# Block transposes on VectorE and moves by DMA for the gated tiles of a fused GateLoop and ELU kernel, with packed features and range tests on ScalarE

## The chip, the cores and the metric

The kernel runs on one core of a Trainium2 chip. A core has five engines with queues of their own: TensorE (PE, with its weight loads shown apart as PEld), VectorE (DVE), ScalarE (ACT), GpSimd (POOL) and SyncE (SP, which here only issues DMAs). They share an on-chip memory of 128 partitions (SBUF); matmul results land in PSUM. Each engine works through its queue in order and waits on semaphores. The metric is the device time of one execution in microseconds (us).

## The reference

A linear recurrence with complex, data-dependent decay, and a two-layer network with ELU behind it:

```python
# q, k, v, a_re, a_im: (batch 4, heads 8, seq 768, head_dim 48), float32
mag = np.sqrt(a_re * a_re + a_im * a_im)
scale = np.minimum(mag, 0.999) / (mag + 1e-06)
a_re_n, a_im_n = (a_re * scale, a_im * scale)
for t in range(S):
    new_re = ar * S_re - ai * S_im
    new_im = ar * S_im + ai * S_re
    S_re, S_im = (new_re + k_t v_t^T, new_im)
    y[:, :, t] = q_t . S_re
x = y as (3072 tokens, 8 * 48)
h = x @ w_in                       # 384 -> 2048
g = np.where(h > 0.0, h, np.exp(np.minimum(h, 0.0)) - 1.0)
out = g @ w_out                    # 2048 -> 384
```

The weights come as float64 words; all else is float32.

## The kernel before, in words

The work is cut into `NU` = 12 units, u = 0 to 11, each of two batch entries (`NB` = 2) and 128 time steps, with 8 heads. The recurrence is done in chunks of 64 steps: the running product of decays is turned into a length (E for q, F = 1/E for k) and an angle, whose cosine and sine stand side by side, so that each head has 48 cosine and 48 sine features. `scaled` multiplies q by E and k by F, and `gated` (L1014) multiplies both by cosine and sine. The result lies in two buffers that all units share, `kg` and `qg`, with time steps on the partitions. Each head takes 2 x 64 columns there, of which 2 x 48 are used and the rest is zero.

For the scores and for the product with the carried state the features must lie on the partitions. `transposed(u, key, n)` (L1034, L1035) does that for one of q or k and one batch entry: eight TensorE transposes of 128x128 into two PSUM tiles, and two ScalarE copies to SBUF. `small` (L1190) multiplies the turned k and q of all heads, in `state_products` (L1075) k and v, `masked` (L1198) applies the causal mask, and `valued_pe` and `carried_pe` (L1111, L1120) give y. ScalarE copies y out, small DMAs bring the heads into place (`seam`, L1241), and the network follows.

From the fourth unit on the network is computed with sums that save products. In `layer_of`, `mult` (L1507) makes twenty groups of matmuls with `w_in`, between which ScalarE (`kept` L1520, `low` L1528 and L1529) and VectorE (`joint` L1523, `whole_of` L1532) add parts together and apply the ELU; `folded` (L1348) prepares sums for `product` (L1370), fourteen groups of matmuls with `w_out`. The results leave by SP (L1398).

Two things are watched on the way. `noted` takes for each unit the smallest real part and the largest imaginary part of the decays (ScalarE with an accumulating output for the first three units, two VectorE reductions, L807 and L810, for the others). `test_fetch` and `test` (L677, L680, L691) read the float64 weights again in 48 pieces and take the smallest high word. `verdict` puts them together and decides whether a general version must run behind.

The order is written by hand: for the first units as a list, then as a plan in which every step has a time in slots, 16 slots to a unit (`put(at, step, ...)`), with a table `SHIFT` of small offsets. The steps are sorted by that time and recorded, and each engine's queue has its instructions in that order. In slots, unit u starts at r = 16 (u - 2). Its gates stand near r + 18 to r + 20, its turned tiles before r + 28.2, where `small` comes. The twenty groups of `mult` of the unit ahead take r + 20 to r + 28, so before the change the transposes of unit u stand among the `mult` groups of unit u - 1. SP issues the loads (`load_a`, `load_qk`, `load_v`), the tests' fetches and the stores in the order of the plan.

Of the kernel before, what the change touches and what calls it, by code (L numbers as in the profile page):

```python
# [505 lines left out]
def kernel(  # L506
# [53 lines left out]
    gates = {key: cst.tile([C, NB, H, 2, HP], FP32, name=key + "g") for key in ("k", "q")}  # L560
# [4 lines left out]
    seen = cst.tile([C, 2 * NU + NR], FP32, name="seen")  # L565
    least, smallest, most = seen[:, 0:NU], seen[:, NU : NU + NR], seen[:, NU + NR :]
    OFF = 3
    off = cst.tile([C, OFF, 2], FP32, name="off")
# [226 lines left out]
    def noted(u):  # L795


        ar, ai = nat[u]["ar"], nat[u]["ai"]
        if u < OFF:
            sq = nat[u]["sq"]  # L800
            for n, (x, scale, bias) in enumerate(((sq, 1.0, most_sq), (ar, -1.0, least_re))):
                nc.scalar.activation(
                    out=sq, in_=x, func=AF.Relu, scale=scale, bias=bias,
                    accum_out=off[:, u, n : n + 1],
                )
            return
        nc.vector.tensor_reduce(  # L807
            out=least[:, u : u + 1], in_=flat(ar), axis=mybir.AxisListType.X, op=ALU.min
        )
        nc.vector.tensor_reduce(  # L810
            out=most[:, u : u + 1], in_=flat(ai), axis=mybir.AxisListType.X, op=ALU.max,
            apply_absolute_value=True,
        )
# [135 lines left out]
    def ends(u):  # L949
# [17 lines left out]
        for i in range(2):  # L967
            nc.gpsimd.dma_start(
                out=x["T"][ds(i * HP, D)].rearrange("p n c h -> p (n c h)"),
                in_=x["ends"].rearrange("n c h d -> d (n c h)"),  # L970
            )
# [33 lines left out]
    def gated(u, part=None, keys=("k", "q")):  # L1005
# [4 lines left out]
        for key in keys if part is None else ("q", "k"):  # L1010
            eng = products(u) if key == "k" else nc.vector
            each = x[key][:, n : n + step].rearrange("p n h d -> p (n h) d")
            to = gates[key][:, n : n + step].rearrange("p n h i d -> p (n h) i d")
            eng.tensor_tensor(  # L1014
                out=to[:, :, :, 0:D], in0=each.unsqueeze(2).to_broadcast([C, step * H, 2, D]),
                in1=x["cs"][:, n * H : (n + step) * H], op=ALU.mult,
            )
# [5 lines left out]
    def transposed(u, key, n):  # L1023
        x = nat[u]
        if u >= PAIRED and key == "k" and n:
            o = new("cs", 1, [C, H, C])
        else:
            o = new(key + "t", 1 + (key == "q"), [C, H, C])
        x[key + "t", n] = o
        for h0 in range(0, H, 4):  # L1030
            t = work([C, 4, C])
            for h in range(4):
                of = gates[key][:, n, h0 + h].rearrange("p i d -> p (i d)")
                nc.tensor.transpose(t[:, h], of, ident)  # L1034
            nc.scalar.copy(out=o[:, h0 : h0 + 4], in_=t)  # L1035
# [19 lines left out]
    def state_products(u, n):  # L1055
# [12 lines left out]
        for h in range(H):  # L1068
            for c, g in enumerate(gs):
                k = gates["k"][ts(c, L), n, h]  # L1070
                parts = [(g[ts(i, HP), h], k[:, i]) for i in range(2)]
                if u == 0:
                    parts = [(g[:, h], k.rearrange("p i d -> p (i d)"))]
# [463 lines left out]
    def verdict():  # L1537

        ones, fit = value(1.0, "ones"), seen[:, 0 : NU + NR]
# [4 lines left out]
            out=least, in0=least, scalar1=LEAST_RE, scalar2=None, op0=ALU.is_ge  # L1544
        )
        nc.vector.scalar_tensor_tensor(
            out=least, in0=most, scalar=LEAST_RE, in1=least, op0=ALU.is_le, op1=ALU.mult
        )
        nc.vector.tensor_scalar(
            out=least[:, 0:OFF], in0=off[:, :, 0], scalar1=0.0, scalar2=None, op0=ALU.is_le  # L1550
# [34 lines left out]
    for n in range(2):  # L1585
        nc.gpsimd.tensor_copy(out=twice[:, ds(n * HP, D)], in_=ident[0:D, 0:D])
    for t in vn:
        nc.gpsimd.memset(t[:, :, HD:], 0.0)
    for t in gates.values():
        nc.gpsimd.memset(t[:, :, :, :, D:], 0.0)  # L1590
# [14 lines left out]
    def warm(n):  # L1605
# [13 lines left out]
        "gated()": 0.05, "gated(None, ('k',))": 0.5, "gated(None, ('k',))@5": -0.2,  # L1619
        "gated(None, ('q',))": 0.45, "gated(None, ('q',))@11": -0.2, "hidden(0,)": 0.05,  # L1620
# [164 lines left out]
    for u in range(2, NU):  # L1785
        r = (u - 2) * SLOTS
        put(r + (8 if u == PAIRED else 4.5 if u == PAIRED + 3 else 1.5), load_a, u)
        put(r + 8, load_v, u)
        put(r + 8, load_qk, u)
# [3 lines left out]
        else:  # L1793
            sq = (r + 7.2, r + 9.6) if u < PAIRED + 4 else (r + 5.08, r + 6)
            noting = r + (15.7 if u != PAIRED + 2 else 17.6)
# [87 lines left out]
```

## Time and profile before

| | |
|---|---|
| median of 3 runs | 645.02 us (643.92 to 645.48) |
| the profiled execution | 644.48 us, its span 642.8 us |
| clock granted to TensorE over that span | 0.996 |
| TensorE busy | 628.7 us |
| VectorE busy | 489.3 us |
| ScalarE busy | 428.5 us |
| GpSimd busy | 159.0 us |
| one unit, from one group of `mult` to the next unit's | 49.1 us |

The span is what the profiler saw between the first and the last instruction; the profiled execution's own time has some 1.7 us more around it. TensorE's row counts a matmul from its start to a modelled end, so a busy TensorE need not be at its peak. A row of a group gives the line, the engine, the operation, the tiles (output, then inputs) and their shapes, the count, and behind the bar the busy time in us and the mean ns of one.

### The profile page before, as it was taken

The numbers are of one execution on the slowest core, as the hardware profiler recorded it, in microseconds if no ns is written. First come the engines' busy times: TensorE is split into PE (matmuls) and PEld (weight loads), VectorE is DVE, ScalarE is ACT, GpSimd is POOL, SyncE is SP. The second block draws the span as 40 slices with busy tenths as digits, with TensorE's granted clock in tenths as the row PEclk, the third lists the DMA queues.
The fourth block names the chain that finished last, engine by engine and source line by source line (L and its number), as shares of the span: only waits on it lengthen the run. The fifth ranks groups of instructions, "written<-read, shape, count | busy, mean of one in ns | idle before, by whom it ended". The sixth has DMA issues, their size and how long they took to land.

```text
span 642.8 us, 17116 instructions
## 1 busy us (share of the span) xinstructions
PE 628.7 (98%) x7236; PEld 576.0 (90%) x7236; DVE 489.3 (76%) x777; ACT 428.5 (67%) x707; POOL 159.0 (25%) x201
## 2 busy tenths in 40 slices
PE   8899999999999999999999999999999999999996
PEld 5788886677899999999999999999999999999995
DVE  5899999869688698698488588588688678664581
ACT  5985573865957777677776776775876776771250
POOL 2000100113124315414414414413604502402000
PEclk9899999999999999999999999999999999999999
DMA  9967569325500712624434244243523352112100
GB/s 182 192 126 135 121 182 205 100 58 87 94 2 16 158 35 73 130 55 97 89 73 96 69 85 100 59 91 96 103 59 82 68 107 64 37 35 62 37 2 31
DMA packets 150706, 56.11 MB, mean 87 GB/s; under 512 B 128948, under 2 KB 142428, under 8 KB 150620
## 3 DMA queue, kind: packets, MB, share of 16 engines
q1 hardware_dynamic: 146880, 53.57, 38.3%
q0 software_dynamic: 3520, 1.20, 1.6%
q8 instruction: 59, 0.97, 0.6%
q14 instruction: 27, 0.22, 0.1%
q10 hardware_dynamic: 220, 0.14, 0.1%
HBM read 48.91 MB, written 4.80 MB: 84 GB/s over the span
## 4 chain that ended last, share of the span: by engine, by line
PE 95%; ACT 2%; DVE 1%; issue 1%; POOL 0%; DVEq 0%; ACTq 0%; POOLq 0%
PE mlp L1370 29%; PE mlp L1507 16%; PE mlp L1261 10%; PE y L1507 9%; PE w L1034 6%; PE w L1075 4%; PE y L1286 3%; PE mlp L1286 3%; PE y L1120 3%; PE y L1190 3%; PE w L848 2%; PE y L1111 2%; PE mlp L1609 1%; PE w L900 1%; PE w L1042 1%
## 5 line engine op out<-in xcount | busy, mean ns | idle before, releaser
L1370 PE MATMUL mlp<-w_out,g 128*128 128x192 f32 x640 | 112.1, 328 | 0.0
L1370 PEld LDWEIGHTS mlp<-w_out,g 128*128 128x128 f32 x640 | 104.3, 190 | 3.4 <-DVE ee L1384 0.6
L1092 POOL TENSOR_TENSOR S<-S,T 128x384 f32<-128x384 f32 x36 | 34.0, 946 | 204.9 <-DVE S L1090 204.9
L1523 DVE TENSOR_TENSOR g<-g,mlp 128x512 f32<-128x512 f32 x45 | 30.9, 686 | 48.9 <-PE mlp L1507 20.8
L1261 PE MATMUL mlp<-x,w_in 128*128 128x256 f32 x288 | 63.8, 380 | 0.0
L1261 PEld LDWEIGHTS mlp<-x,w_in 128*128 128x128 f32 x288 | 54.3, 190 | 8.2
L1348 DVE TENSOR_TENSOR g<-g 128x512 f32<-128x512 f32 x80 | 55.1, 703 | 5.0 <-PE mlp L1370 3.2
L1507 PE MATMUL mlp<-x,w_in 128*128 128x128 f32 x424 | 56.1, 275 | 0.0
L1370 PE MATMUL mlp<-w,g 128*128 128x192 f32 x320 | 54.5, 329 | 0.0
L1370 PEld LDWEIGHTS mlp<-w,g 128*128 128x128 f32 x320 | 51.8, 190 | 0.6
L1507 PEld LDWEIGHTS mlp<-x,w_in 128*128 128x128 f32 x424 | 51.6, 192 | 0.1
L1528 ACT ACTIVATE ee<-g 128x512 f32<-128x512 f32 x63 | 39.5, 626 | 18.2 <-DVE g L1523 16.8
L1241 POOL DMA_DIRECT2D x<-y x62 | 30.6, 501 | 75.8 <-ACT y L1137 39.9
L1532 DVE SCALAR_TENSOR_TENSOR g<-ee,g 128x512 f32<-128x512 f32 x63 | 43.5, 691 | 7.3 <-ACT ee L1529 7.1
L1529 ACT ACTIVATE ee<-ee 128x512 f32<-128x512 f32 x72 | 45.4, 631 | 2.3
L1520 ACT COPY g<-mlp 128x512 f32<-128x512 f32 x36 | 21.1, 586 | 37.5 <-PE mlp L1507 37.4
L1035 ACT COPY qt<-w 128x512 f32<-128x512 f32 x48 | 25.7, 593 | 8.6 <-PE w L1034 8.4
L1251 ACT ACT_TABLE_LOAD x24 | 30.8, 1283 | 0.5
L915 ACT ACTIVATE n<-w 64x384 f32<-64x384 f32 (+1 forms) x60 | 28.1, 486 | 3.9 <-PE w L900 3.0
L1507 PE MATMUL mlp<-x,g 128*128 128x128 f32 x224 | 29.6, 275 | 0.0
L1228 ACT COPY x<-y 128x384 f32<-128x384 f32 x20 | 8.6, 482 | 31.4 <-PE y L1120 31.4
L1507 PE MATMUL y<-x,w_in 128*128 128x128 f32 x216 | 28.6, 275 | 0.0
(226 smaller groups left out, 1416.6 us busy)
## 6 DMA issues: line engine op xcount, KB each, us to landing
w<-in_moe_w_out_dram SPq DMA_DIRECT2D x8, 768.0 KB, 4.7
g<-in_moe_w_in_dram SPq DMA_DIRECT2D x24, 256.0 KB, 3.1
g<-in_moe_w_out_dram SPq DMA_DIRECT2D x24, 256.0 KB, 2.7
w<-in_moe_w_in_dram SPq DMA_DIRECT2D x16, 288.0 KB, 4.0
vn<-in_v_dram SPq DMA_DIRECT2D x24, 192.0 KB, 4.1
q<-in_q_dram SPq DMA_DIRECT2D x11, 384.0 KB, 4.9
k<-in_k_dram SPq DMA_DIRECT2D x11, 384.0 KB
out_dram<-o SPq DMA_DIRECT2D x44, 96.0 KB, 2.4
```

The costliest lines, as they stand in the source:

```text
L1034: nc.tensor.transpose(t[:, h], of, ident)
L1092: eng.tensor_tensor(out=new_s, in0=new_s, in1=wide, op=ALU.mult)
L1251: nc.scalar.preload_act_table_set(name)
L1261: nc.tensor.matmul(t[:, e], lhsT=w_in[:, i, ts(f + e, C)], rhs=x["x"][:, i], start=(i == 0), stop=(i == NI - 1),)
L1286: nc.tensor.matmul(x["o", n], lhsT=x["g", f // 8][:, f % 8, ts(n, C)], rhs=w_out[:, f], start=(f == 0), stop=(f == NF - 1),)
L1348: nc.vector.tensor_tensor(out=S_of(u, k, h), in0=a, in1=b, op=op)
L1370: nc.tensor.matmul(to, lhsT=a[:, m], rhs=b[:, m], start=(first and h == 0 and m == 0), stop=False, skip_group_check=True,)
L1507: nc.tensor.matmul(x["c" + c][:, ts(m, C)], lhsT=a[:, m], rhs=x["mix"][p], start=(p == BANKS[c][0] and m == 0), stop=False, skip_group_che ...
L1523: nc.vector.tensor_tensor(out=part(u, to), in0=part(u, a), in1=part(u, b), op=op)
L1528: nc.scalar.activation(out=e, in_=part(u, of), func=AF.Relu, scale=-1.0)
L1529: nc.scalar.activation(out=e, in_=e, func=AF.Exp, scale=-1.0)
L1532: nc.vector.scalar_tensor_tensor(out=part(u, to), in0=nat[u]["e", to], scalar=-1.0, in1=part(u, of), op0=ALU.add, op1=ALU.max,)
```

## The change

It has four parts.

1. The 96 features of a head are packed: `kg` and `qg` hold 96 columns a head, one behind the other (`kg` with 32 zero columns at its end), and the turned tiles have fixed places (`kt`, `qt`, for both batch entries) whose last 32 partitions are zeroed once. The matmuls keep their shapes; those that took 128 columns of a head now read into the next head's, against rows that are zero.
2. From u = 4, the fifth unit, `flipped` and `moved` stand in place of `transposed`. `flipped` is a VectorE transpose of 128 x 768 in blocks of 32x32 (q in place, k into the buffer that held cosine and sine), four of them in a unit. `moved` copies the blocks to their places: for each of the three groups of 32 features four DMAs, each of 32 partitions by 16 runs of 32 floats, so 24 DMAs in a unit, all issued by SP. The first four units still use TensorE, with the copy of 96 partitions instead of 128.
3. `noted` runs on ScalarE for all units, with a later `verdict` to match.
4. The plan is set anew: `noted` at r + 11, loads of q, k and v from the sixth unit on at r + 10 and r + 12 instead of r + 8, the tests at other slots, and entries of `SHIFT`.

```diff
-    gates = {key: cst.tile([C, NB, H, 2, HP], FP32, name=key + "g") for key in ("k", "q")}
+    F = 2 * D
+    TAIL = C - F
+    gates = {
+        key: cst.tile([C, NB * H * F + n], FP32, name=key + "g")
+        for key, n in (("k", TAIL), ("q", 0))
+    }
+    turned_gates = {key: cst.tile([C, NB, H, C], FP32, name=key + "t") for key in ("k", "q")}
...
-        nc.vector.tensor_reduce(
-            out=least[:, u : u + 1], in_=flat(ar), axis=mybir.AxisListType.X, op=ALU.min
-        )
-        nc.vector.tensor_reduce(
-            out=most[:, u : u + 1], in_=flat(ai), axis=mybir.AxisListType.X, op=ALU.max,
-            apply_absolute_value=True,
-        )
+        ar, sq = nat[u]["ar"], nat[u]["sq"]
+        for n, (x, scale, bias) in enumerate(((sq, 1.0, most_sq), (ar, -1.0, least_re))):
+            nc.scalar.activation(
+                out=sq, in_=x, func=AF.Relu, scale=scale, bias=bias,
+                accum_out=off[:, u, n : n + 1],
+            )
...
+    BL = 32
+
+    def flipped(u, key, n):
+
+        x = nat[u]
+        if n == 0:
+            to = gates["q"]
+            if key == "k":
+                to = new("cs", 1, [C, NB * H, 2, D]).rearrange("p h i d -> p (h i d)")
+            x["flipped", key] = to.rearrange("p (h f) -> p h f", f=F)
+        part = ts(n, H * F)
+        nc.vector.transpose(
+            out=x["flipped", key].rearrange("p h f -> p (h f)")[:, part], in_=gates[key][:, part]
+        )
+        x[key + "t", n] = turned_gates[key][:, n]
+
+    def moved(u, key, b):
+
+        of, to = nat[u]["flipped", key], turned_gates[key].rearrange("p n h t -> p (n h) t")
+        for a in range(C // BL):
+            nc.sync.dma_start(
+                out=to[ts(b, BL), :, ts(a, BL)], in_=of[ts(a, BL), :, ts(b, BL)]
+            )
...
-            for n in range(NB):
-                put(r + 22 + 2 * n, transposed, u, "q", n)
-                put(r + 23 + 2.3 * n, transposed, u, "k", n)
+            if u == PAIRED + 1:
+                for n in range(NB):
+                    put(r + 22 + 2 * n, transposed, u, "q", n)
+                    put(r + 23 + 2.3 * n, transposed, u, "k", n)
+            else:
+                for n in range(NB):
+                    put(r + 19.2 + 0.5 * n, flipped, u, "q", n)
+                    put(r + 21.6 + 0.5 * n, flipped, u, "k", n)
+                for b in range(F // BL):
+                    put(r + 19.75, moved, u, "q", b)
+                for b in range(F // BL):
+                    put(r + 21.6 + 0.55, moved, u, "k", b)
...
-    clear = [SLOTS * n + x for n in range(3, NU) for x in (0.55, 5.2, 7.35, 9.7, 12.3, 14.2)]
+    clear = [SLOTS * n + x for n in range(3, NU) for x in (0.55, 2.4, 4.2, 10.6, 12.4, 14.2)]
```

TensorE, in the middle of the `mult` groups of the seventh unit (`L1507`, in the changed kernel `L1521`), where the eighth unit's tiles were turned (`L1034`). Before:

```order
L1507 MATMUL mlp<-x,w_in 128x128 x4
L1034 MATMUL w<-ident,qg 128x128 x8
L1507 MATMUL mlp<-x,g 128x128 x4
L1507 MATMUL y_3850<-pair,w_in 128x128 x4
L1507 MATMUL y_3849<-x,more 128x128 x4
L1034 MATMUL w<-ident,kg 128x128 x8
L1507 MATMUL mlp<-x,w_in 128x128 x4
```

The same place of the changed kernel:

```order
L1521 MATMUL mlp<-x,w_in 128x128 x4
L1521 MATMUL mlp<-x,g 128x128 x4
L1521 MATMUL y_3780<-pair,w_in 128x128 x4
L1521 MATMUL y_3779<-x,more 128x128 x4
L1521 MATMUL mlp<-x,w_in 128x128 x4
```

The four groups of eight transposes of a unit are gone; the `mult` groups keep their order.

VectorE of the changed kernel, at the same place, from the gate of q (`L1009`, before `L1014`) to the second of the sums that `mult` feeds (`L1537`, before `L1523`); `L1410` is a sum for an output, `L696` a test:

```order
L1009 TENSOR_TENSOR qg_75<-q_3389,cs_3727 128x1536
L1038 STREAM_TRANSPOSE qg_75<-qg_75 128x768
L1410 TENSOR_TENSOR o_3764<-mlp_3408,ee_3542 128x192
L1038 STREAM_TRANSPOSE qg_75<-qg_75 128x768
L696 TENSOR_REDUCE seen_83<-g_1437 128x1
L1537 TENSOR_TENSOR g_3781<-g_3781,mlp_3777 128x4x128
L1038 STREAM_TRANSPOSE cs_3813<-kg_74 128x768 x2
L1537 TENSOR_TENSOR g_3781<-g_3781,mlp_3776 128x4x128
```

Four transposes have come into this queue where before the gate, the sum, the test and the `mult` sums followed each other directly.

SP of the changed kernel, one unit's moves and what stands around them (`out_dram<-o` stores, `g<-in_moe_w_in_dram` a test's fetch):

```order
L1412 DMA out_dram<-o 128x192 x3
L1047 DMA qt<-qg 32x16x32 x8
L682 DMA g<-in_moe_w_in_dram 128x512
L1047 DMA kt<-cs 32x16x32 x12
L1047 DMA qt<-qg 32x16x32 x4
L682 DMA g<-in_moe_w_in_dram 128x512
L609 DMA q<-in_q_dram 128x16x48
L609 DMA k<-in_k_dram 128x16x48
```

The 24 moves stand between the stores and the loads of the next unit's q and k, with one fetch in their midst.

More of the change, by code (lines that the diff above doesn't have):

```diff
@@ L564 @@
     halves = cst.tile([C, 2, C], FP32, name="halves")
[L565 to L568, printed above, removed]
+    seen = cst.tile([C, NU + NR], FP32, name="seen")
+    inside, smallest = seen[:, 0:NU], seen[:, NU:]
+    off = cst.tile([C, NU, 2], FP32, name="off")
     least_re, most_sq = value(LEAST_RE, "least_re"), value(-(LEAST_RE**2), "most_sq")
@@ L1024, in transposed @@
         x = nat[u]
[L1025 to L1029, printed above, removed]
+        x[key + "t", n] = o = turned_gates[key][:, n]
         for h0 in range(0, H, 4):
@@ L1032, in transposed @@
             for h in range(4):
[L1033 to L1035 removed]
+                nc.tensor.transpose(t[0:F, h], gates[key][:, ts(n * H + h0 + h, F)], ident)
+            nc.scalar.copy(out=o[0:F, h0 : h0 + 4], in_=t[0:F])
+    BL = 32
[17 more added lines that the diff above has]
+            )
     def scores(u, n):
@@ L1069, in state_products @@
             for c, g in enumerate(gs):
-                k = gates["k"][ts(c, L), n, h]
-                parts = [(g[ts(i, HP), h], k[:, i]) for i in range(2)]
+                k = gates["k"][ts(c, L), ds((n * H + h) * F, C)]
+                parts = [(g[ts(i, HP), h], k[:, ts(i, HP)]) for i in range(2)]
                 if u == 0:
-                    parts = [(g[:, h], k.rearrange("p i d -> p (i d)"))]
+                    parts = [(g[:, h], k)]
                 for to, of in parts:
@@ L1537, in verdict @@
     def verdict():
-        ones, fit = value(1.0, "ones"), seen[:, 0 : NU + NR]
+        ones, fit = value(1.0, "ones"), seen
         nc.vector.tensor_tensor(
@@ L1543, in verdict @@
         nc.vector.tensor_scalar(
[L1544 to L1550, printed above, removed]
+            out=inside, in0=off[:, :, 0], scalar1=0.0, scalar2=None, op0=ALU.is_le
         )
@@ L1585 @@
     for n in range(2):
-        nc.gpsimd.tensor_copy(out=twice[:, ds(n * HP, D)], in_=ident[0:D, 0:D])
+        nc.gpsimd.tensor_copy(out=twice[:, ds(n * D, D)], in_=ident[0:D, 0:D])
     for t in vn:
         nc.gpsimd.memset(t[:, :, HD:], 0.0)
-    for t in gates.values():
-        nc.gpsimd.memset(t[:, :, :, :, D:], 0.0)
+    nc.gpsimd.memset(gates["k"][:, NB * H * F :], 0.0)
+    for t in turned_gates.values():
+        nc.gpsimd.memset(t[F:C], 0.0)
     nc.gpsimd.memset(seen, 0.0)
```

32 lines of the change are left out of this document (12 added, 20 removed), and 56 rows, old and new, of the table SHIFT.

## The prediction

> **What bounds the kernel now.** I read the page first: the engines' shares, TensorE's 40 slices and the chain that ended last.
>
> ```profile
> span 642.8 us, 17116 instructions
> PE 628.7 (98%) x7236; PEld 576.0 (90%) x7236; DVE 489.3 (76%) x777; ACT 428.5 (67%) x707; POOL 159.0 (25%) x201
> PE   8899999999999999999999999999999999999996
> PE 95%; ACT 2%; DVE 1%; issue 1%; POOL 0%; DVEq 0%; ACTq 0%; POOLq 0%
> ```
>
> TensorE holds 95% of the chain. A busy row alone proves little, since ends are modelled, so I then asked for the stretch that holds all units of the changed kind, and for the chain of waits in one of them, the eighth.
>
> ```profile
> 230.00:600.00 370.00, 370.00 (x4764) 356.21 (x4763) 275.21 (x463) 255.25 (x416) 120.78 (x131) 1.00 0.34 76
> ...
> 360.18 0.89 PE mlp L1507 x8
> 361.07 0.87 PE w L1034 x8
> 361.94 0.89 PE mlp L1507 x8
> ...
> 364.62 0.87 PE w L1034 x8
> ...
> 367.28 0.87 PE w L1034 x8
> ...
> 370.84 0.87 PE w L1034 x8
> ...
> 378.37 1.08 PE w L1075 x64
> 379.45 2.02 PE y L1190 x64
> ```
>
> From 230 to 600 us TensorE has no gap (370.00 of 370.00, clock 1.00), and the eighth unit's four groups of transposes stand in the chain itself, each followed at once by a `mult` group. So TensorE sets the pace, and time taken from it there is time gained, as long as nothing else falls behind.
>
> **The change part by part.** *Transposes off TensorE.* A unit has four groups of 0.87 us, 3.48 us; eight units (the fifth to the twelfth) have them replaced: 27.8 us. From the profiled execution's 644.48 us that leaves **616.7 us**. The first four units keep theirs. Packing changes no matmul's shape: nothing. The price in the other queues follows.
>
> *VectorE.* Here are the prices, and the two stages of the eighth unit: the stretch of `mult` (355.5 to 377.9), the stretch up to the next one, and both together.
>
> ```profile
> 355.50:377.90 22.40, 22.40 (x201) 22.40 (x200) 13.27 (x23) 16.52 (x29) 7.55 (x5) 1.00 0.50 103
> 377.90:404.60 26.70, 26.70 (x439) 24.87 (x439) 24.22 (x41) 18.94 (x30) 9.46 (x13) 1.00 0.29 70
> ...
> 355.50:404.60 49.10, 49.10 (x638) 47.27 (x637) 37.49 (x63) 35.46 (x58) 17.01 (x18) 1.00 0.38 85
> ```
>
> ```profile
> L691 DVE TENSOR_REDUCE seen<-g 128x1 f32<-128x256 f32 x48 | 19.7, 411 | 1.2 <-DMA g<-in_moe_w_out_dram 1.1
> L1014 DVE TENSOR_TENSOR qg<-q,cs 128x1536 f32<-128x1536 f32 x10 | 17.5, 1755 | 0.0
> L50 DVE SCALAR_TENSOR_TENSOR wp<-w,wp 128x768 f32<-128x768 uint32 x16 | 15.3, 957 | 0.4
> L40 DVE TENSOR_SCALAR wf<-w 128x768 uint32<-128x768 uint32 x16 | 9.0, 560 | 0.2
> L807 DVE TENSOR_REDUCE seen<-ar 128x1 f32<-128x768 f32 x9 | 8.5, 943 | 0.0
> ```
>
> No block transpose stands in this trace. Per 128x768 the nearest rows run from 0.56 us (one input, L40) to 0.96 us (L50); twice the elements take 1.76 us (L1014). I take 0.95 us, for most operations of that size lie there, and keep 0.56 and 1.76 as the ends. Four transposes add 3.80 us to a unit; the two range reductions (L807 and its twin on the imaginary part) take away 1.89 us. VectorE then needs 39.4 of a unit's 45.6 us (49.10 less 3.48), where it now needs 37.5 of 49.1. In the `mult` stretch the four transposes come in and one of three tests goes: 13.27 + 3.80 - 0.41 = 16.7 us in a stretch that shrinks to 18.9. In the other stretch 24.22 - 1.89 + 0.41 = 22.7 of 26.7 us. So the cover gets thin in the first and better in the second; nothing is added at 0.95 us.
>
> *ScalarE.* Eight copies a unit go and two range tests come.
>
> ```profile
> L1035 ACT COPY qt<-w 128x512 f32<-128x512 f32 x48 | 25.7, 593 | 8.6 <-PE w L1034 8.4
> L802 ACT ACTIVATE n<-n,most_sq 128x768 f32<-128x768 f32 x3 | 2.8, 928 | 0.0
> ```
>
> 8 x 0.593 = 4.74 us less, 2 x 0.93 = 1.86 us more, 32.6 of 45.6 us: covered. GpSimd keeps its work.
>
> ```profile
> 369.17 1.82 SPq L604 DMA_DIRECT2D k<-in_k_dram  x1
> ...
> 399.44 1.81 POOL L993 TENSOR_TENSOR k<-k,n 128x768 f32<-128x768 f32 x1 [1.89 <-issue]
> ```
>
> The later loads cost nothing: k leaves SP at 369.17 and is first used at 399.44, and three slots more are about 9 us of these 30.
>
> *The moves.* This is the new chain: gate of q, two transposes, 8 moves, gate of k (GpSimd), two transposes, 12 moves, 4 moves of q, then `small`, for which all 24 must have landed. The times below are of the eighth unit; the other rows price a move.
>
> ```profile
> 355.75 1.76 DVE L1014 TENSOR_TENSOR qg<-q,cs 128x1536 f32<-128x1536 f32 x1
> 357.43 0.34 DVE L1396 TENSOR_TENSOR o<-mlp,ee 128x192 f32<-128x192 f32 x1
> ...
> 357.90 3.49 POOL L1014 TENSOR_TENSOR kg<-k,cs 128x1536 f32<-128x1536 f32 x1
> ```
>
> ```profile
> 400.00:401.00 1.00, 1.00 (x8) 1.00 (x7) 0.95 (x3) 0.98 (x2) 1.00 (x1) 1.00 1.08 209
> q1 hardware_dynamic: 146880, 53.57, 38.3%
> L1241 SPq DMA_DIRECT2D x<-y x5: 534/583/597, 40.7 to 149.1; - x5
> x<-y SPq DMA_DIRECT2D x5, 16.0 KB, 1.9
> ```
>
> A move is 512 runs of 128 B, 32 for each of 16 DMA engines. The window at 400 us holds the loads of the decays, in runs of 48 floats, 192 B: at 209 GB/s that is 1089 runs a us, 14.7 ns a run on each engine. At that price a move keeps the engines for 0.47 us. SP takes 0.58 us to issue a copy from SBUF to SBUF (L1241), and that one lands after 1.9 us. The mean packet of the queue, with all its long ones, takes 38.3% of 16 x 642.8 us over 146880: 26.8 ns, 0.86 us a move. So a move costs 0.47 to 0.86 us; I take 0.58, the row of the same kind of copy on the same queue.
>
> The second transpose of q ends near 355.75 + 1.76 + 0.95 + 0.34 + 0.95 = 359.75. SP then issues 24 moves with one fetch of a test among them, 25 x 0.58 = 14.5 us, until 374.25; k's tiles are ready by 357.90 + 3.49 + 2 x 0.95 = 363.3, before SP has done q's eight and the fetch (365.0), so they hold up nobody. With 1.9 us to land it is 376.15. The scores, now at 379.45, come 3.48 us earlier, at 375.97. **The moves land 0.2 us late**, 1.4 us over eight units. At 0.47 us a move they land 2.6 us early. Behind the moves SP holds only a fetch and the loads of q, k and v, with some 20 us to spare. The seam's own DMAs (x<-y) run on GpSimd's queue.
>
> The sum is 644.5 - 27.8 + 1.4 = 618.1 us, and since the median of the runs shown, 645.02 us, is 0.5 above the profiled execution, **618.6 us** for the median.
>
> **The rivals.** *VectorE becomes the bound of the `mult` stretch.* At 1.76 us a transpose VectorE needs 13.27 + 7.04 - 0.41 = 19.9 us in 18.9, and it can't fill the first of its waits there (the gate of k is ready only at 361.4): some 2 us a unit, 16 us in all, and 633 us. For it speaks that its four transposes stand ahead of the sums `mult` waits for; against it the 4 us to spare in the other stretch, and that the 128x768 rows above are all under 1 us. [...]
>
> *The moves come late: slower than before.* Each us by which they land after the scores are due is a us of TensorE in every unit. The gain of 3.48 us is gone when 25 issues take 375.97 + 3.48 - 1.9 - 359.75 = 17.8 us, that is from **0.71 us a move**. At the queue's mean packet, 0.86 us, the last lands at 383.15, 7.2 us late: 616.7 + 57 = 674 us. Against it speak the 14.7 ns of the 192 B runs; for it, that no row shows many short runs from SBUF to SBUF. [...]
>
> *The moves come a little late:* between 0.62 and 0.70 us a move, 1 to 3 us a unit, 625 to 641 us. *No gain:* the products wait for sums of ScalarE and VectorE that the transposes had covered, 3.48 us in each unit, and the time stays near 645 us. Against it: the same stretch loses 4.74 us of ScalarE's copies.
>
> **How the numbers follow.** The forecast, 614 to 624 us, gets 0.58; VectorE as the bound 0.17; moves a little late 0.06; no gain 0.03; moves too late and slower 0.13; better than 614 us 0.03, since outside 230 to 600 us TensorE has 14.1 us of idle time (642.8 - 628.7) of which other edits might close a few. From 613 to 638 us lie nearly all of the first two and most of the third, about 0.8. About 0.3%, 2 us, is what a measurement of this kernel can tell from no change. Faster: 0.58 + 0.17 + 0.06 + 0.03 = 0.84; same 0.03; slower 0.13.
>
> **What would show it.** The unit's period at 45.6 us and TensorE without gaps at the scores (L1204 in the changed kernel) would show the main step right. A wait of TensorE for the moves there shows the second rival or the third, with its length in us a unit; the block transpose's mean ns decides the first; waits of `mult` for VectorE or ScalarE show the fourth. The moves' rows must show 0.5 to 0.6 us from one issue to the next. Wrong would be the whole argument if a unit's period fell by less than 2 us with none of these waits.

## The result, and the profile after

The changed kernel takes **660.83 us** (median of 4 runs, 659.26 to 665.07) against 645.13 us of the kernel before: a ratio of 1.0257, interval 1.0207 to 1.0308. It is 2.6% slower; forecast were 618.6 us, 613 to 638. The profiled execution took 661.54 us. Its page (engine: busy us, share, instructions; then tenths of 40 slices; then the chain that ended last):

```profile
span 659.8 us, 16884 instructions
PE 618.0 (94%) x6980; PEld 560.7 (85%) x6980; DVE 501.8 (76%) x789; ACT 411.9 (62%) x679; POOL 161.8 (25%) x202
PE   8899999999999789989989989979989989999995
PEclk9899999999999989989989989999999989999998
PE 51%; SPq 15%; DVE 10%; DMA 6%; POOL 6%; issue 6%; ACT 5%; DVEq 0%; ACTq 0%; POOLq 0%
```

TensorE no longer carries the chain: 51% instead of 95%. SP's queue alone holds 15%, and the granted clock dips once in seven of the eight changed units (eights in the last row but one). The eight changed units, by windows from the start of one unit's `mult` to the next (us, busy time of each engine, clock, DMA share, GB/s); the last row is the sum over all eight:

```profile
209.40:263.70 54.30, 48.17 (x607) 45.67 (x606) 44.20 (x71) 33.91 (x55) 16.44 (x18) 0.97 0.55 105
...
365.10:416.00 50.90, 47.69 (x605) 45.47 (x605) 39.18 (x65) 33.56 (x55) 17.35 (x19) 0.97 0.62 113
...
sum 405.60, PE 379.58 PEld 362.37 DVE 307.85 ACT 251.30 POOL 127.04; mean PE 47.45 PEld 45.30 DVE 38.48 ACT 31.41 POOL 15.88
```

Before, these eight took 390.9 us without a gap of TensorE (the same columns, all eight in one window):

```profile
208.20:599.10 390.90, 390.90 (x4949) 377.11 (x4948) 291.47 (x489) 271.45 (x443) 126.80 (x134) 1.00 0.35 79
```

Less the 27.8 us of transposes, 363.1 us of TensorE's work are left, 45.4 us a unit on average. They take 405.6: 26.0 us in which TensorE is idle, and 16.5 us in which it is busy for longer. The whole miss lies here. What the idle time waits for, on TensorE's matmul queue in that stretch (us, times, longest):

```profile
PE y L1204 <- DMA qt<-qg: 7.9, 8, 1.6
PE y L1521 <- ACT g L1534: 7.4, 6, 2.1
PE mlp L1521 <- ACT g L1534: 3.7, 2, 3.3
PE w L1089 <- issue: 2.1, 1, 2.1
PE y L1204 <- DMA vn<-in_v_dram: 1.9, 1, 1.9
...
```

Three waits, not one: 7.9 us for the moves at the scores (L1204), 11.1 us for ScalarE's copies in the stretch of `mult` (L1521), and 4.0 us that have to do with the loads: 1.9 us for a load of v, and 2.1 us put to issue (the engine waited for nothing that the profile shows), on which e1 and e5 bear. The rest are 3.0 us for VectorE.

**The moves.** The eighth unit (start 365.1 us) on SP's queue and on TensorE, in order of time (start, us, operation, idle before it), and the clock of the 3.4 us behind the scores' start:

```profile
369.07 6.19 SPq L1047 DMA_DIRECT2D qt<-qg  x8
375.36 0.56 SPq L682 DMA_DIRECT2D g<-in_moe_w_in_dram  x1
376.02 7.98 SPq L1047 DMA_DIRECT2D kt<-cs  x12
384.05 2.64 SPq L1047 DMA_DIRECT2D qt<-qg  x4
386.79 1.45 SPq L682 DMA_DIRECT2D g<-in_moe_w_in_dram  x1
388.28 0.44 SPq L609 DMA_DIRECT2D q<-in_q_dram  x1
```

```profile
385.48 1.15 PE L1089 MATMUL w<-vn,kg 64*64 64x48 f32 x64
387.38 0.30 PE L1204 MATMUL y<-qt,kt 128*64 128x64 f32 x2 [0.75 <-DMA qt<-qg]
389.31 2.92 PE L1204 MATMUL y<-qt,kt 128*64 128x64 f32 x62 [1.63 <-DMA qt<-qg]
```

```profile
390.40:393.80 3.40, 3.40 (x98) 3.28 (x94) 1.38 (x2) 1.13 (x2) 0.00 (x0) 0.53 1.36 208
```

The 25 issues take 17.6 us (369.07 to 386.69), the last move lands 2.6 us later, at 389.31, and the scores, ready at 386.63, wait. Then the clock stands at half for 3.4 us. The moves' rows, with the time from issue to landing:

```profile
L1047 SPq DMA_DIRECT2D qt<-qg x96: 585/627/1749, 214.2 to 588.7; - x96
...
DMA to landing us min/median/max: 2.1/2.3/3.9
```

**ScalarE's copies.** Each row here stands for one engine in the same unit: VectorE's block transposes of k wait for GpSimd's gate, VectorE's sum behind them is late, ScalarE's activation waits for that sum, the copies queue behind the activation, and TensorE waits for a copy out of the tile that it writes next:

```profile
370.78 1.84 DVE L1038 STREAM_TRANSPOSE cs<-kg 128x768 f32<-128x768 f32 x2 [0.88 <-POOL kg L1009]
372.54 0.65 DVE L1537 TENSOR_TENSOR g<-g,mlp 128x512 f32<-128x512 f32 x1
```

```profile
373.23 0.63 ACT L1542 ACTIVATE ee<-g 128x512 f32<-128x512 f32 x1 [1.07 <-DVE g L1537]
...
374.43 0.57 ACT L1534 COPY g<-y 128x512 f32<-128x512 f32 x1
```

```profile
375.05 1.16 PE L1521 MATMUL y<-x,w_in 128*128 128x128 f32 x8 [0.83 <-ACT g L1534]
```

### The profile page after: what moved, and what is told of

It reads as the page before. It is cut to its first block, busy times and chain, and to the rows that moved or that the text cites. A ratio compares the mean times of both kernels' runs of the same rounds, so it can differ in the third digit from the quotient of the medians.

```text
span 659.8 us, 16884 instructions
## 1 busy us (share of the span) xinstructions
PE 618.0 (94%) x6980; PEld 560.7 (85%) x6980; DVE 501.8 (76%) x789; ACT 411.9 (62%) x679; POOL 161.8 (25%) x202
## 4 chain that ended last, share of the span: by engine, by line
PE 51%; SPq 15%; DVE 10%; DMA 6%; POOL 6%; issue 6%; ACT 5%; DVEq 0%; ACTq 0%; POOLq 0%
PE mlp L1384 17%; SPq L1047 10%; PE mlp L1275 9%; PE mlp L1521 4%; POOL kg L1009 4%; PE y L1300 3%; PE y L1204 3%; PE y L1134 3%; SPq L609 2%; PE mlp L1300 2%; PE w L1089 2%; DMA qt<-qg 2%; PE y L1521 2%; SPq L660 2%; PE w L1024 2%
## 5 line engine op out<-in xcount | busy, mean ns | idle before, releaser
L1384 PE MATMUL mlp<-w_out,g 128*128 128x192 f32 x640 | 113.7, 331 | 0.0
L1384 PEld LDWEIGHTS mlp<-w_out,g 128*128 128x128 f32 x640 | 105.7, 192 | 3.4 <-DVE ee L1398 0.6
L1521 PE MATMUL mlp<-x,w_in 128*128 128x128 f32 x424 | 56.3, 276 | 3.3 <-ACT g L1534 3.3
L1521 PEld LDWEIGHTS mlp<-x,w_in 128*128 128x128 f32 x424 | 51.6, 192 | 3.7 <-ACT g L1534 3.5
L1537 DVE TENSOR_TENSOR g<-g,mlp 128x512 f32<-128x512 f32 x45 | 30.5, 677 | 21.7 <-PE mlp L1521 20.6
L1543 ACT ACTIVATE ee<-ee 128x512 f32<-128x512 f32 x72 | 45.4, 630 | 2.3
L1204 PE MATMUL y<-qt,kt 128*64 128x64 f32 x576 | 25.8, 256 | 12.3 <-DMA qt<-qg 7.9
L1521 PE MATMUL y<-x,w_in 128*128 128x128 f32 x216 | 30.2, 284 | 7.4 <-ACT g L1534 7.4
L1204 PEld LDWEIGHTS y<-qt,kt 128*64 128x64 f32 x576 | 23.8, 168 | 13.8 <-issue 5.6
L1521 PEld LDWEIGHTS y<-x,w_in 128*128 128x128 f32 x216 | 27.0, 197 | 8.7 <-ACT g L1534 8.7
L1521 PE MATMUL mlp<-x,g 128*128 128x128 f32 x224 | 30.4, 280 | 0.4 <-ACT g L1534 0.4
```

The lines of the kernel that those rows point to most:

```text
L1204: nc.tensor.matmul(t[n][ts(c, L), ts(h, L)], lhsT=x["kt", n][:, h, ts(c, L)], rhs=x["qt", n][:, h, ts(c, L)], start=True, stop=True,)
L1384: nc.tensor.matmul(to, lhsT=a[:, m], rhs=b[:, m], start=(first and h == 0 and m == 0), stop=False, skip_group_check=True,)
L1521: nc.tensor.matmul(x["c" + c][:, ts(m, C)], lhsT=a[:, m], rhs=x["mix"][p], start=(p == BANKS[c][0] and m == 0), stop=False, skip_group_che ...
L1543: nc.scalar.activation(out=e, in_=e, func=AF.Exp, scale=-1.0)
```

## The experiments

All times stand beside runs of the kernel before on the same chip (medians 644.2 to 645.4 us). The runs were made in five groups on different chips (e1 to e4, e5 to e8, e9 to e11, e12 to e14, e15), so across groups the ratios compare better than the times.

| run | what differs from the changed kernel | us | ratio to before, interval |
|---|---|---|---|
| e1 | all tiles turned by TensorE | 653.9 | 1.0131 [1.0098, 1.0164] |
| e2 | matmuls without use ahead of the scores | 661.6 | 1.0275 [1.0239, 1.0310] |
| e3 | k by TensorE, q moved | 638.6 | 0.9905 [0.9886, 0.9925] |
| e4 | k's moves on GpSimd's queue | 642.7 | 0.9960 [0.9942, 0.9979] |
| e5 | e1, loads early | 646.7 | 1.0031 [1.0010, 1.0053] |
| e6 | e3, loads early | 639.3 | 0.9900 [0.9882, 0.9918] |
| e7 | e4, k's block transposes later | 642.6 | 0.9981 [0.9952, 1.0011] |
| e8 | e7, loads early, q's moves in one piece | 669.1 | 1.0350 [1.0311, 1.0389] |
| e9 | e7, loads behind the scores | 636.1 | 0.9875 [0.9846, 0.9905] |
| e10 | loads behind the scores | 656.9 | 1.0205 [1.0171, 1.0238] |
| e11 | e9, first unit by TensorE | 639.8 | 0.9904 [0.9864, 0.9943] |
| e12 | k's block transposes later | 665.3 | 1.0250 [1.0179, 1.0322] |
| e13 | e9, second half of k by TensorE | **631.6** | 0.9832 [0.9769, 0.9895] |
| e14 | e9, two of k's moves on SP | **633.4** | 0.9814 [0.9788, 0.9840] |
| e15 | e8, a fetch ahead of the moves | 656.6 | 1.0154 [1.0116, 1.0191] |

### The parts of the change: e1, e2, e3, e4

**e1** turns every unit's tiles on TensorE again; packing, range tests and the new order stay. The first half of q is turned three slots later than its old entry says, so that it stands behind its gate.

```diff
-            if u == PAIRED + 1:
+            if u > PAIRED:
...
-                    put(r + 22 + 2 * n, transposed, u, "q", n)
+                    put(r + 22 + 2 * n + (3 if n == 0 and u > PAIRED + 1 else 0), transposed, u, "q", n)
```

> The changed kernel with the tiles of all units turned by TensorE again; packing, range tests on ScalarE and the new plan stay. Theory A (the moves are issued too slowly and land late, TensorE waits at the scores and its granted clock falls to half for 3.4 us after each wait) and theory B (the block transposes in VectorE's queue hold up sums, ScalarE's copies and so the mult groups) both expect the time of before, 643 to 648 us, and no half-clock stretch within the units. Theory C (packing, range tests or the plan cost the time) expects 652 to 661 us.

653.9 us: 8.5 us are lost without any move, as theory C expected, which left open whether packing, range tests or the plan did it. In the eight units TensorE's only gaps lie at the small matmuls (L1089), five of them, 6.4 us in all, put to issue, while the loads of q, k and v run, which the change has put there. SP and TensorE in the eighth unit:

```profile
386.69 4.04 SPq L605 DMA_DIRECT2D vn<-in_v_dram  x2
```

```profile
391.44 0.66 PE L1089 MATMUL w<-vn,kg 64*64 64x48 f32 x27 [1.01 <-issue]
```

**e2** puts 12 matmuls without use (24 rows of the trace) ahead of the scores, in the eight units; their result is overwritten.

```diff
+        for _ in range(12 if u > PAIRED + 1 else 0):
+            nc.tensor.matmul(t[0][:, 0:C], lhsT=ident, rhs=ident, start=True, stop=True)
```

> The changed kernel with 12 dummy matmuls of 128x128 (some 2.6 us) between the first state products and the scores of the fifth to the twelfth unit, which fill TensorE's wait and change no data path. If the wait itself brings the clock down, the mean granted clock goes from 0.977 to above 0.99 and the time from 661 to 647 to 652 us, although the moves land as late as before. If the clock falls for another reason, the clock stays at 0.97 to 0.98 and the time at 660 to 670 us.

661.6 us, the same as the changed kernel, so the 647 to 652 us forecast for a clock brought down by the wait did not come. But the clock's mean is 0.991 in the profiled run (0.983 to 0.991 in the four) instead of 0.977, as that theory has it, and the wait for the moves is all but gone from TensorE's queue:

```profile
385.09 2.94 PE L1202 MATMUL y<-ident 128*128 128x128 f32 x24
387.96 2.08 PE L1206 MATMUL y<-qt,kt 128*64 128x64 f32 x64
```

The matmuls take 2.94 us where the wait and the half clock stood. TensorE is busy for 392.0 us in the eight units, less 8 x 2.94 it is 368.5: 11 us less than the 379.6 of the changed kernel. That is what the half clock costs, and its mean says much the same (0.996 before, 0.977 after: 0.019 x 659.8 = 12.5 us), as do the trace's seven dips in that stretch, of 3.41 us each (half of 7 x 3.41 is 11.9 us). The time stays because the 23.5 us of added matmuls replace only 13.0 us of idle time (26.0 in the changed kernel, 13.0 left here), and the 10.5 us on top eat what the clock gives. Of the 16.5 us in which TensorE was busy for longer, some 4.4 us are not the clock's: e9, with the clock at 1.00 all through these units, is still busy for 367.5 us against 363.1. What they are stays open.

**e3** turns k by TensorE and moves q alone, 12 moves instead of 24.

```diff
-                    put(r + 21.6 + 0.5 * n, flipped, u, "k", n)
+                    put(r + 23 + 2.3 * n, transposed, u, "k", n)
-                for b in range(F // BL):
-                    put(r + 21.6 + 0.55, moved, u, "k", b)
```

> The changed kernel with k turned by TensorE (as in the first four units) and only q by VectorE and 12 moves. Theory A: 12 moves and a fetch of 0.67 us are out some 9 us after the gate of q, 5 us or more before the scores; no wait there, clock above 0.99, and half of the 27.8 us comes off: 629 to 634 us. Theory B, if the two transposes of q alone do it: above 640 us.

638.6 us, faster than both kernels, and between the two forecasts. Most units take 47.6 us, where half of the gain would leave 47.36: no move is late there, and TensorE gets what it is spared. The first two take 50.1 and 49.5 us, which keeps the time above 634.

**e4** leaves all 24 moves and issues k's from GpSimd's queue.

```diff
-            nc.sync.dma_start(
+            (nc.gpsimd if key == "k" else nc.sync).dma_start(
```

> The changed kernel with the 12 moves of k issued by GpSimd, beside the 12 of q on SP. GpSimd sits idle for some 15 us there. Theory A: if GpSimd needs no more than 0.9 us a move, all land before the scores are due, the clock stays above 0.99, and the time is 618 to 630 us. Theory B: the waits of the mult groups for ScalarE stay as they are and the time is 640 us or more even though the scores wait for nothing. If GpSimd needs above 1.2 us a move, its moves are late in their turn and the time is above 655 us.

642.7 us, 18 us faster than with one queue, and where theory B had it. TensorE's waits for the moves shrink from 7.9 to 0.8 us; those for ScalarE's copies stay (7.0 and 3.4 us). So one queue for 24 moves was the largest single price, and it is a price of issuing.

### Loads and the wait behind GpSimd: e5, e6, e7, e8

**e5** and **e6** are e1 and e3 with the loads where they stood before the change, in the stretch of `mult`.

(Here and below, the loads' own entries in the table of shifts go too, and from e7 on that of `flipped`, where k's block transposes move.)

```diff
-        put(r + (8 if u < PAIRED + 3 else 10), load_qk, u)
-        put(r + (8 if u < PAIRED + 3 else 12), load_v, u)
+        put(r + 8, load_qk, u)
+        put(r + 8, load_v, u)
```

> All tiles turned by TensorE as in e1, but the loads of q, k and v stand where they stood before the change (in the stretch of the mult groups) instead of in the time of the small matmuls of the sums and scores. Theory A (loads that run beside the dense small matmuls starve TensorE of instructions: 16.6 us of idle put to issue at L1089 in e1, 4.7 us at the same line before): the loss of e1 goes, 644 to 647 us, and idle put to issue at L1089 falls below 7 us. Rival (the 96 packed features, the range tests on ScalarE or the new order cost e1 its 8.5 us): 652 to 656 us as in e1.

> q by VectorE and DMA, k by TensorE as in e3, with the loads of q, k and v back in the stretch of the mult groups. Theory A: the steady units of e3 take 47.6 us against 47.36 that half the gain leaves, so little is to be had in them, and 1 to 3 us in the first two units: 635 to 638 us. Rival (the loads, on the queue of the moves and on the same 16 DMA engines, delay q's moves, and the scores wait): 640 to 650 us.

e5: 646.7 us, 7.2 us less than e1; the idle time put to issue at L1089 falls from 6.6 to 0.7 us on TensorE's matmul queue (1.0 before the change). So the place of the loads cost e1 nearly all its loss, and packing, range tests and the rest of the order some 2 us (the interval says 0.6 to 3.4). e6: 639.3 us, no gain over e3 and between the two forecasts, though in e3 the loads run beside the same small matmuls.

What comes late are TensorE's own instructions, by the author's reading of the kept traces; which engine a packet serves they don't say. Among their DMA records are those of the queue that the page of the profile calls instruction (q8, 59 packets of 16 KB in e1). In each of e1's five gaps (fifth to ninth unit) such a packet starts 0.9 to 1.8 us after the scores do, and TensorE goes on 1.4 to 1.6 us after the packet's end, each time with 27 or 28 of the 64 matmuls left. In the same units of e5 and of the kernel before, the packet starts within 0.2 us of the scores' start, and no gap is longer than 0.5 us; so it is in e1's tenth unit, where the loads stand earlier. In e3 the packets fall elsewhere in TensorE's order, and only the first of the eight units has a gap there (1.1 us).

**e7** is e4 with k's two block transposes one sum later in VectorE's order.

```diff
-                    put(r + 21.6 + 0.5 * n, flipped, u, "k", n)
+                    put(r + 22.25 + 0.05 * n, flipped, u, "k", n)
-                    put(r + 21.6 + 0.55, moved, u, "k", b)
+                    put(r + 22.35, moved, u, "k", b)
```

> k's moves issued by GpSimd as in e4; k's two block transposes stand one sum later in VectorE's order, so that the sum on which ScalarE waits runs ahead of them. Theory B (the block transposes wait for GpSimd's gate of k, the sum behind them is late, ScalarE's activation and the copies behind it too, and TensorE waits before its next mult group: 22.2 us of idle put to ScalarE's copies in e4): that idle falls below 10 us and the time to 630 to 637 us. Rival (the wait only moves to the next sum, or k's moves, now later, hold up the scores): 641 us or more.

Half of it came. The waits for ScalarE's copies fall from 10.4 to 0.7 us, so the path through VectorE and ScalarE is shown. The time stays at 642.6 us, as the rival had it, for the scores, reached earlier, now wait, for moves of both tiles, for VectorE and for a fetch:

```profile
PE y L1204 <- DMA kt<-cs: 3.1, 3, 1.4
PE y L1204 <- DVE g L1546: 2.1, 2, 1.2
PE y L1204 <- DMA qt<-qg: 2.1, 2, 1.2
```

**e8** adds the early loads (as in e5) and puts q's twelve moves in one piece ahead of them.

```diff
-        "moved('q', 1)": 3.0,
```

> e7 with q's twelve moves in one piece and the loads of q, k and v behind them in the stretch of the mult groups. Theories A and B together: beside the idle put to ScalarE's copies, that put to issue at L1089 and L1204 (9.8 us in e4) falls below 5 us, 622 to 632 us, below the 638.6 us of e3. Rival (loads and moves share the DMA engines, the moves land later and the scores wait): no faster than e7, 640 us or more.

669.1 us, the slowest of all. In the seventh unit VectorE waits 7.27 us in its test of the weights (L696) for a fetch that stands in SP's queue behind the twelve moves; the sum behind that test is late, and the scores wait for it. SP, VectorE and TensorE:

```profile
324.19 10.80 SPq L1047 DMA_DIRECT2D qt<-qg  x12
335.09 1.57 SPq L682 DMA_DIRECT2D g<-in_moe_w_in_dram  x1
```

```profile
343.63 0.42 DVE L696 TENSOR_REDUCE seen<-g 128x1 f32<-128x256 f32 x1 [7.27 <-DMA g<-in_moe_w_in_dram]
```

```profile
345.31 4.07 PE L1204 MATMUL y<-qt,kt 128*64 128x64 f32 x64 [4.62 <-DVE g L1537]
```

Over the eight units VectorE waits 50.7 us for such fetches, against 8.2 us in the changed kernel and 1.1 us before.

### Loads behind the scores: e9, e10, e11

**e9** is e7, **e10** the changed kernel, each with the loads of q, k and v behind one more fetch for a test of the weights ("check fetch" in the expectations), which SP reaches only after the scores; **e11** is e9 with the first changed unit's tiles turned by TensorE.

```diff
-        put(r + (8 if u < PAIRED + 3 else 10), load_qk, u)
-        put(r + (8 if u < PAIRED + 3 else 12), load_v, u)
+        put(r + (8 if u < PAIRED + 3 else 12.45), load_qk, u)
+        put(r + (8 if u < PAIRED + 3 else 12.45), load_v, u)
```

```diff
-            if u == PAIRED + 1:
+            if u <= PAIRED + 2:
```

> e7 (k's moves issued by GpSimd, k's block transposes one sum later), with the loads of q, k and v put behind one more check fetch, so that they are issued some 11 us later, after the scores, from the sixth unit on. Theory D (in e7 the loads, issued from 426.9 us on, share the DMA engines with the last moves, whose issue ended at 426.6 us: the last move lands only at 431.9 us, and 24 us of idle before the scores, L1204, come of it; 8.0 us more are put to issue at L1089): the idle before L1204 falls below 8 us and the clock rises above 0.99; 622 to 632 us, faster than the 638.6 us of e3. Rival (the moves are slow by themselves: issue and landing fill the 18 us, or the loads, now late, hold up ScalarE's and GpSimd's work on k): 638 to 645 us.

> The kernel after, all moves on SP, with nothing altered but the place of the loads of q, k and v: issued after the scores from the sixth unit on. Theory D: the idle put to issue at L1089 and L1204 (13.4 us) goes below 6 us and the waits for the moves shrink, but SP's queue still ends its moves about where the scores are due and the half clock stays: 646 to 654 us. Rival (loads play no part where the moves are late by SP's queue alone): 658 to 662 us.

> e9 with the tiles of the first of the eight changed units (u = 4) still turned by TensorE. Theory: the first unit's one-off loss (51.4 us in e7 against 45.6 us of work) goes for 3.5 us of turns: 1 to 3 us faster than e9. Rival: the loss goes to the next unit, and the kernel is 3 us slower than e9.

e9: 636.1 us, 6.5 us less than e7; it is 4 us above the forecast and 2 us below the rival's. The clock's mean is 0.994 in the profiled run. The largest wait left at the scores is 4.9 us for k's moves, and the DMA engines' share is 1.15 and 1.17 there (windows of the ninth unit; the second number from the right):

```profile
415.00:417.00 2.00, 2.00 (x21) 2.00 (x20) 1.59 (x3) 0.98 (x2) 1.96 (x4) 1.00 1.15 227
417.00:419.00 2.00, 2.00 (x21) 2.00 (x20) 2.00 (x4) 1.62 (x3) 0.80 (x2) 1.00 1.17 129
```

e10: 656.9 us, between the two forecasts and only 4 us less than the changed kernel, a difference that the intervals don't separate: where SP alone issues all moves, the loads are a small part at most. e11: 639.8 us, not to be told from e9 by the intervals. Its numbers bear on time alone: the first half of q in that one unit is turned ahead of its gate, so it holds what the unit before left. The first unit takes 48.6 us instead of 51.5, but it starts 2.7 us later, and the seven behind it take 3.9 us more, so nothing is gained. What the first unit loses stays open.

### What ends last: e12, e13, e14, e15

**e12** is the changed kernel with the edit of e7 alone; **e13** is e9 with the second half of k's tiles by TensorE, so that k's moves carry half; **e14** is e9 with two of k's moves given to SP. The first edit below is from e13, the second from e14, both in part.

```diff
+                    put(r + 22.25, flipped, u, "k", n) if n == 0 else put(r + 25.3, transposed, u, "k", n)
...
+                out=to[ts(b, BL), ds(0, part), ts(a, BL)], in_=of[ts(a, BL), ds(0, part), ts(b, BL)]
```

```diff
+            (nc.gpsimd if key == "k" and not (b == 2 and a > 1) else nc.sync).dma_start(
```

> The kernel after, all moves on SP, with nothing altered but k's two block transposes one sum later in VectorE's order, as in e7. Theory E (SP's queue of 24 moves ends at a fixed time after the unit's start, whatever TensorE does before): the 23.9 us of idle put to ScalarE's copies go, but they come back before the scores, and the time stays at 657 to 664 us. Rival (that wait costs time of its own): 645 to 652 us.

> e9 with the second half of k's tiles turned by TensorE again, so that k's twelve moves carry half as much: 1 of the 4 groups of turns (0.87 us) is back in each of the eight units, 7.0 us in all. Theory F (in e9 the moves of two queues fill the 16 DMA engines, share 1.03 to 1.21 from 415 to 423 us, and the last lands 1 to 2.5 us late): the waits before the scores go and the units take 46.5 us; with the first unit as in e9, 630 to 634 us. Rival (what e9 still waits for is VectorE's sums): 637 to 643 us.

> e9 with the last two of k's twelve moves issued by SP ahead of q's last four. Theory F (DMA engines full): no gain, 634 to 640 us. Rival (GpSimd's queue is what ends last, since it stalls after its ninth move): the last move is issued 1.5 us earlier, and the time is 626 to 632 us.

e12: 665.3 us (656.9 to 669.1), not to be told from the changed kernel. The waits for ScalarE's copies are gone (11.1 to 0.7 us), and those for the moves grow from 7.9 to 12.3 us: on one queue, SP's last move sets the time, and what TensorE loses ahead of it costs nothing more.

```profile
PE y L1204 <- DMA qt<-qg: 12.3, 10, 2.8
```

e13: 631.6 us. The eighth unit, and what TensorE waits for in all eight:

```profile
352.80:399.90 47.10, 46.85 (x613) 44.87 (x613) 38.56 (x64) 34.76 (x57) 24.23 (x31) 1.00 0.61 113
```

```profile
PE mlp L1522 <- ACT g L1535: 0.7, 1, 0.7
PE w L1090 <- issue: 0.3, 1, 0.3
```

Units of 47.1 us (46.5 by the sum), the clock at 1.00 and hardly a wait, and the time as forecast; that it is faster than e9 the intervals don't show, for one of its four runs took 638.7 us. e14: 633.4 us, 2.8 us less than e9; the intervals just don't meet (up to 0.9840 against from 0.9846). In e9 the waits at the scores name GpSimd's moves, and in the ninth unit GpSimd issues its last one 2.8 us after SP's, so its queue did end last there; but the time of e14 lies between the two forecasts, and GpSimd itself waits 4.2 us for its own earlier moves to land (e9), so that the DMA engines have a share in it isn't excluded. e13 and e14 can't be told apart; both are faster than the kernel before by some 1.8%.

**e15** is e8 with one test fetch of each unit ahead of q's moves.

```diff
-(0.55, 2.4, 4.2, 10.6, 12.4, 14.2)
+(0.55, 2.4, 3.6, 10.6, 12.4, 14.2)
```

> e8 with one check fetch of each unit put ahead of q's twelve moves instead of behind them. Theory G (a fetch behind the moves lands late, VectorE's test waits for it, the sums behind the test are late, and TensorE waits at the scores): VectorE's waits for fetches fall from 50.7 us to below 15 us, TensorE's wait put to VectorE's sums at L1204 from 26 us to below 8 us, and the time to 635 to 648 us. Rival (the loads hold up the last moves themselves): 660 us or more, the wait then named by the moves.

656.6 us, 12.5 less than e8, between the two forecasts, and about half of the 26.5 us that e8 lost against e7. VectorE's waits for fetches fall from 50.7 to 19.9 us, and TensorE's for VectorE's sums from 26.2 to 7.5. These 7.5 us all lie in the first of the eight units, where a fetch still comes behind the moves and VectorE waits 10.0 us for it. Of the rest, k's moves are named with 5.0 us and the loads of q with 3.5, so the loads between moves and scores seem to cost as well.

## Why the prediction was wrong, step by step

- **TensorE sets the pace, and 3.48 us a unit taken from it are gained "as long as nothing else falls behind".** Right as a condition: e3 and e13, where little is late, come within 0.3 and 0.7 us a unit of what their share of the groups leaves, in most units. The changed kernel does not meet the condition.
- **The block transpose at 0.95 us.** Right: medians of 0.96 (k) and 0.97 us (q), 32 in all. The first rival, VectorE as the bound, falls by it: VectorE is busy for 307.9 of 405.6 us.
- **"I take 0.58" for a move, 25 issues in 14.5 us, 1.9 us to land.** This term was mis-sized, and it is the one that decides. The median issue is 0.627 us and stands 0.04 us from the next; q's first eight take 0.77 us each. 25 issues take 17.6 us and the median landing 2.3. Put into the prediction's own sum, 359.75 + 17.6 + 2.3 = 379.65, 3.7 us after the scores are due, and the gain is gone: 616.7 + 8 x 3.7 + 0.5 = 647 us. So corrected, the sum has the last move land 24.2 us behind the unit's start (379.65 - 355.50), and so does the trace (389.31 - 365.10). Measured were 0.70 us a move. That is the upper end of the third rival (0.62 to 0.70, chance 0.06), and the longer landing takes it over the line of the second (0.71, chance 0.13), which named this place. Both got little, for the price was read from five short copies (L1241) and from runs of 192 B on other paths, though no row showed the operation itself. e3 (half the moves) and e4 (a second queue) show it.
- **The clock.** It was in no term. Behind the waits at the scores and at the small matmuls around them the clock falls to half for 3.41 us, seven times in the eight units, 11 to 12 us in all (e2). So a move that is late by 1 us can cost 2.7, as an estimate (half of 3.4 us on top). This is the larger part of the way from 647 to 661 us.
- **"k's tiles are ready by ... 363.3 ... so they hold up nobody."** True for SP, wrong for VectorE: the block transposes wait there for GpSimd's gate (8.2 us), and the sums behind them go on to ScalarE and TensorE. It was priced only within the first rival. With one queue it comes out of the wait for the moves (e12); with two queues it is gone in e7 and e9, but no run has the late loads of e9 without it, so what it is worth there isn't shown.
- **"The later loads cost nothing."** Their data had 30 us to spare; what they run beside was left out. Their place costs e1 7.2 us (e5), e7 6.5 us (e9), and the changed kernel some 4 (e10), which is not clear of the noise. Among what they run beside are the packets of the instruction queue, which in e1's gaps start 0.9 to 1.8 us after the scores do.
- **"Behind the moves SP holds only a fetch"** with time to spare. In the changed kernel VectorE waits 8.2 us for such fetches, and in e8 this one fetch, behind four more moves, costs 12.5 us (e15).
- **ScalarE at 32.6 of 45.6 us.** Right in size (251.3 us, 31.4 a unit) and of no help: its waits in order mattered, not its busy time.

## What to carry to other kernels

Price a new operation that is issued dozens of times in a unit by a run of its own, or keep the range open on the side where it decides: here 0.12 us a move and 0.4 us of landing stood, in the prediction's own sum, between a gain of 4% and none. The last item of SP's queue was a deadline here (12.3 us of waits of the scores for q's moves in e12), and whatever is moved into that queue or behind its waits (a fetch, a load, a transpose that waits for another engine) must be followed to the engine that waits next. Where a transfer can't carry all of the work in time, let it carry a part: on SP's queue alone, half of the tiles (e3) made the kernel 1% faster than before, and all of them 2.6% slower.

## What the runs showed of the hardware

- **Half clock came by windows of 3.41 us, and short waits that added up to 2.2 us in one were enough.** In the eighth unit of the changed kernel two waits of 0.75 and 1.63 us around the first two matmuls of the scores were followed by half clock; in the ninth unit of e9 waits of 1.58 and 0.93 us at the same place were not. The seven dips of the changed kernel start at 236.59, 287.79, 338.99, 390.19, 444.80, 530.13 and 591.57 us, whole multiples of 3.413 us apart, and so do the dips within each of the 17 traces. Counted by these windows, the two cases differ: the first has 2.2 us of idle time in one window, the second 0.85 and 1.7 us in two. In all traces from 120 to 600 us, half clock followed on each of the 28 windows at full clock with 1.9 us of idle time or more, on 6 of 23 with 1.4 to 1.9 us, and on 4 of 2290 with less; in the changed kernel's trace alone on 6 of 6, none of 2, and 1 of 125. The windows that hold these waits, and the one behind them (the changed kernel, then e9; the clock is the third number from the right):

```profile
386.78:390.19 3.41, 1.18 (x32) 1.11 (x34) 1.24 (x3) 3.35 (x7) 0.83 (x1) 1.00 0.55 120
390.19:393.60 3.41, 3.41 (x95) 3.29 (x92) 1.38 (x2) 1.34 (x2) 0.00 (x0) 0.50 1.35 212
```

```profile
420.87:424.28 3.41, 2.56 (x74) 2.21 (x72) 3.38 (x7) 3.31 (x7) 0.40 (x1) 1.00 0.94 143
424.28:427.69 3.41, 1.75 (x51) 1.67 (x53) 1.27 (x3) 3.35 (x7) 0.83 (x1) 1.00 0.03 8
427.69:431.11 3.42, 3.42 (x95) 3.30 (x91) 2.80 (x6) 1.27 (x3) 0.83 (x1) 1.00 0.02 5
```

- **With one queue issuing, the DMA engines had time to spare; with two, their share went above 1.** With copies of 512 runs of 128 B from SBUF to SBUF the share of the DMA engines is 0.65 from SP alone (the row below, a stretch of k's moves in the changed kernel) and 1.17 from SP and GpSimd (e9, 417 to 419 us), where k's median landing grows from 2.3 to 5.5 us. With SP alone issuing was the larger part (17.6 us in a unit, 2.3 us to land), and the second queue took off 18 us (e4).

```profile
381.00:383.00 2.00, 2.00 (x21) 2.00 (x20) 2.00 (x5) 1.94 (x4) 0.00 (x0) 1.00 0.65 97
```

- **Loads beside small matmuls left gaps on TensorE.** Loads of 1.2 MB beside the matmuls of L1089, 64 in 1.15 us, left TensorE five gaps of 0.9 to 1.9 us that no engine or transfer is named for (e1), each behind a packet of the instruction queue that came 0.9 to 1.8 us into the scores. In the stretch of `mult` the same loads left one gap, of 0.2 us (e5), and in e3, where they run beside the same matmuls but the packets fall elsewhere, one of 1.1 us.
